# Moving weight loads, one weight conversion and parts of two scan units in a fused SSD scan and SiLU feed-forward kernel

## The chip, the core and the metric

The kernel runs on one core of a Trainium2 chip. The core has TensorE (PE in the profile, with PEld for its weight loads), VectorE (DVE), ScalarE (ACT), GpSimd (POOL) and SyncE (SP, which here only issues transfers); 16 DMA engines move data between HBM and SBUF. The metric is the device time of one execution in microseconds; lower is better. A kernel's time is the median of several runs, and the profile is one further execution.

## The reference

Two blocks one after the other. The first is a chunked state-space scan (Mamba-2's SSD) over 4 batches x 8 heads x 768 steps, with 32 values per head and 16 states; the second is a feed-forward layer on 3072 tokens of 256 values: a product with w_in (256 x 2048), SiLU, and a product with w_out (2048 x 256). All is float32.

```python
for c in range(nc):                       # chunks of the sequence
    cum = np.cumsum(la, axis=-1)          # la = log(clip(a, 1e-6, 1))
    L = np.exp(cum[:, :, :, None] - cum[:, :, None, :]) * causal
    CB = np.einsum('bhin,bhjn->bhij', Cc, Bc)
    y_intra = np.einsum('bhij,bhjd->bhid', CB * L, xc)
    y_inter = np.einsum('bhin,bhnd->bhid', Cc, state) * np.exp(cum)[:, :, :, None]
    y[:, :, sl] = y_intra + y_inter
    decay_from_j = np.exp(cum[:, :, -1:] - cum)
    Bx = np.einsum('bhjn,bhjd->bhjnd', Bc, xc) * decay_from_j[:, :, :, None, None]
    state = np.exp(np.sum(la, axis=-1))[:, :, None, None] * state + np.sum(Bx, axis=2)
x = y.transpose(0, 2, 1, 3).reshape(3072, 256)
h = x @ w_in
out = (h * (1.0 / (1.0 + np.exp(-h)))) @ w_out
```

## The kernel before

**Units.** The scan works in units of 256 steps of one batch, with chunks of 64 steps; units 0 to 2 are batch 0, unit 3 starts batch 1, twelve in all. A unit u takes these steps, each a function: `f_P` (DVE: running products of a from the tile pz, result pfx), `f_Ek` or `f_E1` (DVE: two scans that build the decay matrix E from the tile ab, one for each half k), `f_B` (B times the last column of E, result BT), `f_TP` or `f_T` (transposes of B and C into bh and ct, on TensorE or on DVE), `f_T2` (ACT: C for even and odd heads, ce), `f_C` (C times pfx, result cw), `f_G` (TensorE: C times B into a PSUM tile of four banks called gy or dp), `f_D0` (TensorE: BT times x), `f_M` (DVE: E times the products of `f_G`, written over E, for each half k), `f_S` (DVE: four states in a row, st), `f_SM` (ACT: copies of the states for even and odd heads, sm), `f_Y` (TensorE: the unit's output) and `f_X` (ACT: the output from PSUM into SBUF, xf).

**Weights.** w_in and w_out are taken in 16 blocks, n from 0: blocks 0 to 7 are 256 columns of w_in each, blocks 8 to 15 are 256 rows of w_out each. They arrive as float64, and the kernel makes float32 of them itself: `load_w(n)` brings 512 KB into a raw tile (a pool of six buffers, so block n + 6 waits until block n is converted), `w_size(n)` makes two tiles of it on ACT (wu from the upper words, wv from the lower), and `w_bits(n)` joins them with three DVE instructions and one addition, which is on POOL unless `adder` is DVE. In the program's text for the later blocks a step is one letter and a number: s is `w_size`, b is `w_bits`, a is `w_bits` with the addition on DVE, r is the load; h, l and d make the split parts of the weights with which the second phase computes.

**Order.** There is no scheduler: each engine executes its instructions in the order in which the program emits them. Phase one, to about 72 us, runs the scans of units 0 to 3 and the feed-forward of units 0 and 1 in plain float32: `f_s1(u, j)` is the product of unit u with block j into half a PSUM tile hp (two buffers) with SiLU on ACT behind it (gT), and `f_s2(j)` the product with block 8 + j. `busy(n)` issues n products of zeros, fillers whose result nobody reads. The text strings in `steps` say which steps of units 2 and 3 and of the weights follow each `f_s1`: "2:TB" is transposes and B of unit 2, "2:a" loads ab of unit 3. From 72 us a steady loop over the remaining unit pairs with split weights follows, which the change does not touch.

**Queues.** Nearly all loads go through SP, which issues them one by one in program order. `f_A2` (POOL) clips a of the later batches and `f_A3` stores it to scratch in HBM (a_in, a_zero), from where pz (`load_pa`) and ab (`load_ab`) of unit 3 and later are read back broadcast over partitions. In the stretch that the change touches SP's order before is: w4, x of unit 2, `f_A3`'s three stores, w5, B and C of unit 3 (eight loads, `load_bcx(3, "c")`), w6, pz and ab of unit 3, w7, B and x of unit 3, w8 and on.

Of the kernel before, what the change touches and what calls it, by code (L numbers as in the profile page):

```python
# [33 lines left out]
def kernel(  # L34
# [22 lines left out]
    nc = tc.nc  # L57

    batch, H, S, D = x.shape
# [26 lines left out]
    def block(name, dtype=FP32):  # L86

        return blk.tile([128, 512], dtype, name=name, tag="blk", bufs=NB)

    def half(name):  # L90
        return ps_h.tile([128, 512], FP32, name=name, tag="h")
# [46 lines left out]
    def load_x(u, q, ks=(0, 1)):  # L138
        b, t0 = at(u)
        if u not in xt:  # L140
            xt[u] = loads.tile([128, 2, H, D], FP32, name="xt", bufs=2)
        for k in ks:
            q.dma_start(out=xt[u][:, k], in_=x[b, :, t0 + 128 * k:t0 + 128 * k + 128].rearrange("h p d -> p h d"))
# [28 lines left out]
    def two(t):  # L172
        return t.rearrange("p (k f) -> p k f", k=2)

    def load_w(n, q):
        j = n % 8
        src = wi[:, :, j * WF:(j + 1) * WF] if n < 8 else wo[:, 2 * j:2 * j + 2]
        if src.dtype == FP32:
            w32[n] = block("w32")
            q.dma_start(out=two(w32[n]), in_=src)  # L180
            return
        t = raw[n] = quad.tile([128, 2, WF, 2], U32, name="raw", tag="quad")
        q.dma_start(out=t.rearrange("p k f two -> p k (f two)"), in_=src.bitcast(U32))
# [65 lines left out]
    load_n(0, 0, nc.scalar)  # L249
    load_a(0)  # L250
    load_x(0, nc.sync)
    for n in range(2):
        load_w(n, nc.sync)
    load_a(1)

    def f_A():
# [13 lines left out]
    def f_A2(first):  # L270

        r = slice(0, NC1)
        nc.gpsimd.tensor_scalar(out=(acl if first else acz)[r], in0=acl[r], scalar1=1.0, scalar2=1e-6, op0=ALU.min, op1=ALU.max)
        if not first:
            nc.gpsimd.memset(acz[r, :, 0:1], 0.0)

    def f_A3():

        r = slice(0, NC1)
        nc.sync.dma_start(out=a_in[:, :, 0:1].rearrange("h c t -> c h t"), in_=misc[r, 0:H].rearrange("p (h t) -> p h t", t=1))  # L280
        nc.sync.dma_start(out=a_in[:, :, 1:].rearrange("h c t -> c h t"), in_=acl[r])
        nc.sync.dma_start(out=a_zero, in_=acz[r])
# [12 lines left out]
    def busy(n, small=0, t=None):  # L295
        t = half("zero") if t is None else t
        for i in range(n):
            nc.tensor.matmul(out=t, lhsT=idle[:, 0:128], rhs=idle, start=True, stop=True)
        for i in range(small):
            nc.tensor.matmul(out=t[:64, :64], lhsT=idle[:, 0:64], rhs=idle[:, 64:128], start=True, stop=True)  # L300
# [67 lines left out]
    def f_Ek(u, k, hs=slice(0, H)):  # L368
        scan_E(u, H * k + hs.start, hs.stop - hs.start, ab.pop((u, k, hs.start))[:, hs])
# [8 lines left out]
    def f_B(u, engine=nc.vector, ks=slice(0, 2)):  # L378
        if u not in BT:
            BT[u] = sc.tile([128, 2, H, N], FP32, name="BT")  # L380
        engine.tensor_tensor(out=BT[u][:, ks], in0=bn[u][:, ks],
                             in1=E[u][:, ks, :, Q - 1:Q].to_broadcast([128, ks.stop - ks.start, H, N]), op=ALU.mult)
# [7 lines left out]
    def f_TP(u):  # L390

        d = new_dp(u)
        for i, t in enumerate((bn[u],) if u == 0 else (bn[u], tbc.pop(u))):
            for k in range(2):
                nc.tensor.transpose(out=d[:, 2 + i, 256 + 128 * k:384 + 128 * k],
                                    in_=t[:, k].rearrange("p h n -> p (h n)"), identity=ident)
        BH[u] = sc.tile([128, UT], FP32, name="bh")
        if u > 0:
            nc.scalar.activation(BH[u], d[:, 2, 256:512], AF.Copy)
        if u == 1:  # L400
            CT[u] = sc.tile([128, UT], FP32, name="ct")
            nc.scalar.activation(CT[u], d[:, 3, 256:512], AF.Copy)
        elif u > 0:
            CT[u] = d[:, 3, 256:512]
# [6 lines left out]
    def f_C(u, engine=nc.vector):  # L411
        CW[u] = sc.tile([128, UT], FP32, name="cw")
        engine.tensor_tensor(out=CW[u].rearrange("p (c t) -> p c t", t=Q),
                             in0=CT.pop(u).rearrange("p (c t) -> p c t", t=Q), in1=PFX[u][:, :, 1:], op=ALU.mult)
# [6 lines left out]
    def f_D0(u, ts=(0, 1, 2, 3)):  # L421
        last = u % UPB == UPB - 1
        bt = BT[u].rearrange("p k h n -> p k (h n)")
        xc = xt[u].rearrange("p k h d -> p k (h d)")
        if 0 < u <= UPB:
            d = [two(acc("d")[:, 0:128]) for c in range(2)]
        else:
            d = [two(new_dp(u)[:, c, 256:384]) for c in range(2)]
        for t in ts[:3 if last else 4]:
            k, c = divmod(t, 2)  # L430
            for g in range(4):
                nc.tensor.matmul(out=d[c][32 * g:32 * g + 32, k],
                                 lhsT=bt[64 * c:64 * c + 64, k, 32 * g:32 * g + 32],
                                 rhs=xc[64 * c:64 * c + 64, k, 64 * g:64 * g + 64], start=True, stop=True,
                                 tile_position=(64 * c, 32 * g), skip_group_check=True)
        BX[u] = d
        if 3 in ts:
            BT.pop(u)
# [61 lines left out]
    def f_X(u):  # L500

        XF[u] = block("xf")
        y = GY.pop(u)
        for w in range(2):
            nc.scalar.activation(two(XF[u])[:, w].rearrange("p (k c t) -> p c k t", k=2, c=2),  # L505
                                 y[:, 2 * w:2 * w + 2, 0:128].rearrange("p c (k t) -> p c k t", k=2), AF.Copy)
# [21 lines left out]

    GT, OA = {}, {}

    def f_s1(u, j):
        hp = two(half("hp"))
        for i in range(2):
            for kc in range(KC):
                nc.tensor.matmul(out=hp[:, i], lhsT=two(w32[j])[:, kc, 128 * i:128 * i + 128],  # L535
                                 rhs=two(XF[u])[:, kc], start=(kc == 0), stop=(kc == KC - 1))
        GT[u, j] = block("gT")
        nc.scalar.activation(two(GT[u, j]), hp, AF.Silu)
        if j == 7:
            XF.pop(u)  # L540
# [196 lines left out]
    w_size(1, "u")  # L737
    busy(2, 10)
    f_Y(0)
    busy(4)  # L740
    f_X(0)
    w_size(1, "v")
    load_w(4, nc.sync)
# [4 lines left out]
    for e in range(2):  # L748
        f_T2(1, e)
    f_Ek(1, 0)  # L750
    f_Ek(1, 1)
    f_s1(0, 0)
    f_B(1, nc.gpsimd)
    f_G(1)
    f_s1(0, 1)
    f_D0(1)
    f_M(1, 0)
    f_P(1)
    f_C(1, nc.gpsimd)
    f_P0(2, nc.gpsimd)  # L760
    f_A2(True)
    f_A2(False)
    f_A3()
    load_w(5, nc.sync)
    load_bcx(3, "c")
    load_w(6, nc.sync)
    load_pa(3, nc.sync)
    f_M(1, 1)
    w_size(2)
    f_S(1)  # L770
    f_SM(1)
    w_size(3, "u")
    busy(6)
    f_Y(1)
    f_X(1)
    w_size(3, "v")
    w_bits(2, adder=nc.vector)

    def stage(u, what):
        for c in what:  # L780
            if c == "L":
                load_unit(u)
            elif c == "a":
                load_ab(u + 1, nc.sync)
            elif c == "n":
                load_n(u, 0, nc.sync)
            elif c == "x":
                load_x(u, nc.sync)
            elif c == "T":
                if 0 < u < UPB:  # L790
                    f_TP(u)
                else:
                    f_T(u, 0)
                    f_T(u, 1)
                f_T2(u, 0)
                f_T2(u, 1)
            elif c == "P":
                f_P(u)
            elif c in "12":
                f_E1(u, int(c) - 1, 2)  # L800
            elif c == "B":
                f_B(u, nc.gpsimd if u == 2 else nc.vector)
            elif c == "C":
                f_C(u)
            elif c == "D":
                f_G(u)
                f_D0(u)
            elif c == "M":
                f_M(u, 0)
                f_M(u, 1)  # L810
            elif c == "S":
                f_S(u)
            elif c == "s":
                f_SM(u)
            elif c == "Y":
                f_Y(u)
                f_X(u)
            elif c == "h":
                f_xh(u)
            elif c == "l":  # L820
                f_xl(u)
            elif c == "d":
                f_xd(u)
# [4 lines left out]
    def todo(text):  # L828

        for step in text.split():  # L830
            if ":" in step:
# [3 lines left out]
            n = int(step[1:].split(".")[0])  # L835
            {"b": w_bits, "s": w_size, "h": w_h, "l": w_l, "d": w_d, "a": partial(w_bits, adder=nc.vector), "v": partial(w_d, vector=True), "m": f_s2, "p": s1_d, "r": load_r}[step[0]](n)

    steps = ((1, 0, "2:P12"), (1, 1, "2:TB a3 s4 2:a r7"), (0, 2, "2:CD 3:nx b4 s5 r8"), (1, 2, "2:SsM r9"),
             (0, 3, "b5 s6 r10"), (1, 3, "2:Y 3:T r11"), (0, 4, "3:P1 b6 s7 r12"), (1, 4, "3:C2B"), (0, 5, "b7 r13 s8"),
             (1, 5, "3:DSsM"), (0, 6, "b8 r14 s9"), (1, 6, "3:Y h0 l0"), (0, 7, "b9 r15 s10 s11"), (1, 7, "b10 s12 2:h"))  # L840
    for u, j, text in steps:
        f_s1(u, j)
        todo(text)
# [117 lines left out]
```

## Time and profile before

| What | Value |
| --- | --- |
| Three timed runs | 331.94, 333.86, 334.7 us |
| Their median | 333.86 us |
| Profiled execution, its time | 330.76 us |
| Its span, first to last instruction | 329.0 us |
| Mean granted TensorE clock | 0.998 |
| Moved by DMA, mean | 31.87 MB, 97 GB/s |

The page also cuts the span into 40 slices of 8.2 us; a digit is the busy share in tenths:

```profile
PE   8989999999999999999999999999999999999995
DVE  7989598987796988996866996866996863574443
ACT  3655669946688898667757657767657756656561
POOL 5532135785012131240202240202240202000000
PEclk9999999999999999999999999999999999999999
DMA  6997999797783952444600454600442000021001
```

The first eight slices hold what the change touches. A time given with an instruction below is its start in us from the start of the span. "A <- B" in a wait means that A's engine stood still until B, as far as the profile can tell; with several conditions it names the one that it saw come last, which can be another than the true one. On SP a line is the issuing of a transfer, not the transfer.

### The profile page before, as it was taken

Reading aid. Unit: us, or ns where it says so; the run is one execution under the profiler, and the core shown is the slowest. Engines: PE = TensorE matmul, PEld = TensorE weight load, DVE = VectorE, ACT = ScalarE, POOL = GpSimd, SP = SyncE. Lnnn points to the kernel's source line nnn. Section 1 sums busy time; section 2 is a strip of 40 time slices with the busy share of each in tenths; the row PEclk is TensorE's granted clock in tenths of the full one; section 3 lists DMA queues with packets and bytes.
Section 4 is the critical chain, followed back from the end, with each engine's and each line's share of the span. In section 5 each row is a group of like instructions: output and inputs, shape, how many; then the busy total and the mean of one; then the engine's idle time right before and its main releaser. Section 6 shows DMA issues by size and latency. Waiting matters only on the chain.

```text
span 329.0 us, 7993 instructions
## 1 busy us (share of the span) xinstructions
PE 321.2 (98%) x3226; PEld 260.5 (79%) x3229; DVE 251.4 (76%) x414; ACT 220.7 (67%) x422; POOL 76.5 (23%) x79
## 2 busy tenths in 40 slices
PE   8989999999999999999999999999999999999995
PEld 4557878888878788778788778788778788899995
DVE  7989598987796988996866996866996863574443
ACT  3655669946688898667757657767657756656561
POOL 5532135785012131240202240202240202000000
PEclk9999999999999999999999999999999999999999
DMA  6997999797783952444600454600442000021001
GB/s 132 242 188 192 226 287 292 153 183 134 159 139 84 160 99 53 99 73 100 118 3 0 84 95 92 119 3 0 94 86 49 2 2 0 0 36 31 2 0 64
DMA packets 92724, 31.87 MB, mean 97 GB/s; under 512 B 76480, under 2 KB 83392, under 8 KB 92688
## 3 DMA queue, kind: packets, MB, share of 16 engines
q1 hardware_dynamic: 87376, 25.60, 35.7%
q0 software_dynamic: 2944, 5.38, 9.1%
q10 hardware_dynamic: 2368, 0.39, 0.7%
q8 instruction: 25, 0.41, 0.6%
q14 instruction: 11, 0.09, 0.1%
HBM read 22.79 MB, written 3.32 MB: 79 GB/s over the span
## 4 chain that ended last, share of the span: by engine, by line
PE 87%; DMA 5%; DVE 4%; issue 2%; SPq 1%; POOL 1%; ACT 1%; DVEq 0%
PE hp L571 23%; PE hp L563 11%; PE oa L612 9%; PE oa L613 9%; PE b L643 9%; PE oa L548 8%; PE hp L535 3%; PE b L638 2%; PE b L621 2%; PE oa L621 2%; PE gy L495 2%; PE gy L446 2%; DMA bn<-in_B_dram 2%; DMA raw<-in_moe_w_in_dram 2%; PE gy L486 2%
## 5 line engine op out<-in xcount | busy, mean ns | idle before, releaser
L565 ACT ACTIVATE hp<-hp 128x512 f32<-128x512 f32 x80 | 46.6, 582 | 71.4 <-PE hp L563 71.3
L585 DVE TENSOR_TENSOR gl<-g,gh 128x512 fp32r<-128x512 f32 x62 | 42.7, 689 | 49.9 <-ACT gh L581 47.0
L571 PE MATMUL hp<-xh,wh 128*128 128x512 f32 x160 | 65.4, 408 | 0.0
L589 DVE SCALAR_TENSOR_TENSOR gd<-gh,g 128x512 fp32r<-128x512 f32 x80 | 59.5, 747 | 5.2 <-ACT gh L581 5.2
L571 PE MATMUL hp<-xl,wl 128*128 128x512 f32 x160 | 62.7, 392 | 0.0
L585 POOL TENSOR_TENSOR gl<-g,gh 128x512 fp32r<-128x512 f32 x18 | 29.3, 1630 | 121.7 <-ACT gh L581 115.8
L581 ACT ACTIVATE gh<-g 128x512 fp32r<-128x512 f32 x80 | 50.6, 632 | 2.8
L612 PE MATMUL oa<-gh,wh 128*128 128x512 f32 x128 | 50.0, 390 | 0.0
L613 PE MATMUL oa<-gl,wl 128*128 128x512 f32 x128 | 49.9, 390 | 0.0
L563 PE MATMUL hp<-xd,wd 128*128 128x512 f32 x160 | 49.6, 391 | 0.0
L579 ACT ACTIVATE g<-hp 128x512 f32<-128x512 f32 x80 | 47.5, 594 | 0.6 <-PE hp L571 0.6
L571 PEld LDWEIGHTS hp<-xh,wh 128*128 128x128 f32 x160 | 30.0, 188 | 8.8 <-ACT hp L565 2.6
L563 PEld LDWEIGHTS hp<-xd,wd 128*128 128x128 f32 x160 | 30.0, 188 | 6.6
L643 PE MATMUL b<-gd,wd 128*128 128x512 f32 x128 | 34.5, 389 | 0.0
L571 PEld LDWEIGHTS hp<-xl,wl 128*128 128x128 f32 x160 | 30.1, 188 | 4.8
L357 DVE TENSOR_TENSOR_SCAN E<-ab,diag 128x512 f32<-128x512 f32 (+1 forms) x26 | 29.4, 1165 | 1.9 <-DMA ab<-a_zero 1.6
L535 PE MATMUL hp<-xf,w 128*128 128x256 f32 x128 | 29.8, 385 | 0.6 <-ACT xf L505 0.5
L548 PE MATMUL oa<-gT,w 128*128 128x256 f32 x128 | 28.4, 379 | 0.0
L612 PEld LDWEIGHTS oa<-gh,wh 128*128 128x128 f32 x128 | 24.0, 188 | 5.1
L613 PEld LDWEIGHTS oa<-gl,wl 128*128 128x128 f32 x128 | 24.0, 188 | 5.1
L643 PEld LDWEIGHTS b<-gd,wd 128*128 128x128 f32 x128 | 24.0, 188 | 5.1
L535 PEld LDWEIGHTS hp<-xf,w 128*128 128x128 f32 x128 | 23.6, 190 | 4.5 <-ACT xf L505 0.6
(107 smaller groups left out, 460.0 us busy)
## 6 DMA issues: line engine op xcount, KB each, us to landing
ab<-a_zero SPq DMA_DIRECT2D x18, 256.0 KB
raw<-in_moe_w_in_dram SPq DMA_DIRECT2D x8, 512.0 KB
raw<-in_moe_w_out_dram SPq DMA_DIRECT2D x8, 512.0 KB
wl<-w POOLq DMA_DIRECT2D x16, 256.0 KB, 4.1
xt<-in_x_dram SPq DMA_DIRECT2D x24, 128.0 KB
out_dram<-ot SPq DMA_DIRECT2D x40, 64.0 KB
tbc<-in_C_dram SPq DMA_DIRECT2D x40, 32.0 KB
bn<-in_B_dram SPq DMA_DIRECT2D x20, 64.0 KB
```

The lines of the kernel that those rows point to most:

```text
L535: nc.tensor.matmul(out=hp[:, i], lhsT=two(w32[j])[:, kc, 128 * i:128 * i + 128], rhs=two(XF[u])[:, kc], start=(kc == 0), stop=(kc == KC - 1))
L548: nc.tensor.matmul(out=OA[0][m][:, UT * u:UT * u + UT], lhsT=two(w32[8 + j])[:, i, 128 * m:128 * m + 128], rhs=two(GT[u, j])[:, i], start= ...
L563: nc.tensor.matmul(out=HP[s], lhsT=two(WD[f // 2])[:, kc, 128 * (f % 2):128 * (f % 2) + 128], rhs=XD[P][:, kc], start=(kc == 0), stop=Fals ...
L565: nc.scalar.activation(HP[s], HP[s], AF.Copy, scale=HALF / UP)
L571: nc.tensor.matmul(out=HP[s], lhsT=two(w[f // 2])[:, kc, 128 * (f % 2):128 * (f % 2) + 128], rhs=x_[P][:, kc], start=False, stop=(kc == KC ...
L579: nc.scalar.activation(G[s], HP.pop(s), AF.Silu, scale=UP)
L581: nc.scalar.activation(GH[s], G[s], AF.Copy, scale=DOWN)
L585: engine.tensor_tensor(out=GL[s], in0=G[s], in1=GH[s].bitcast(FP32), op=ALU.subtract)
L589: nc.vector.scalar_tensor_tensor(out=GD[s], in0=GH[s].bitcast(FP32), scalar=1.0 + 1.0 / HALF, in1=G.pop(s), op0=ALU.mult, op1=ALU.subtract)
L612: nc.tensor.matmul(out=OA[P][m], lhsT=two(WH[n])[:, r, ms], rhs=gh, start=(f == 0), stop=False)
L613: nc.tensor.matmul(out=OA[P][m], lhsT=two(WL[n])[:, r, ms], rhs=gl, start=False, stop=(f == NF - 1))
L643: nc.tensor.matmul(out=B2[P][:, m], lhsT=two(WD[n])[:, r, 128 * m:128 * m + 128], rhs=gd, start=(fresh and s == tiles[0]), stop=True, skip ...
```

## The change

Seven edits, all in phase one:

- Unit 1's `f_B` is issued as two halves, each directly behind the scan that it needs, ahead of `f_s1(0, 0)`.
- Unit 1's `f_D0` is issued between the two halves of the product `f_s1(0, 1)`, not behind it; `f_s1` gets an argument for that.
- Fillers: six, not four, before `f_X(0)`; five, not six, before `f_Y(1)`; two new ones before `f_X(1)`.
- Unit 2's transposed C is copied from PSUM to SBUF on ACT, as unit 1's was, and `f_C(2)` moves from DVE to POOL, directly behind `f_B(2)`.
- SP's order: w5 ahead of the three stores of a; w6 and w7 ahead of B and C of unit 3 (before: w6 behind them, w7 behind ab of unit 3).
- `w_bits(6)` does its addition on DVE, not on POOL.
- `w_size(8)` and `w_size(9)` each move one product later: behind `f_SM(3)` and behind `f_X(3)`.

The first hunk only writes a loop out; it changes no instruction.

```diff
-    for n in range(2):
-        load_w(n, nc.sync)
+    load_w(0, nc.sync)
+    load_w(1, nc.sync)
...
-        if u == 1:
+        if u in (1, 2):
             CT[u] = sc.tile([128, UT], FP32, name="ct")
             nc.scalar.activation(CT[u], d[:, 3, 256:512], AF.Copy)
...
-    def f_s1(u, j):
+    def f_s1(u, j, between=None):
         hp = two(half("hp"))
         for i in range(2):
+            if i == 1 and between:
+                between()
             for kc in range(KC):
...
     f_Y(0)
-    busy(4)
+    busy(6)
     f_X(0)
...
     f_Ek(1, 0)
+    f_B(1, nc.gpsimd, slice(0, 1))
     f_Ek(1, 1)
+    f_B(1, nc.gpsimd, slice(1, 2))
     f_s1(0, 0)
-    f_B(1, nc.gpsimd)
     f_G(1)
-    f_s1(0, 1)
-    f_D0(1)
+    f_s1(0, 1, lambda: f_D0(1))
...
     f_A2(False)
+    load_w(5, nc.sync)
     f_A3()
-    load_w(5, nc.sync)
+    load_w(6, nc.sync)
+    load_w(7, nc.sync)
     load_bcx(3, "c")
-    load_w(6, nc.sync)
     load_pa(3, nc.sync)
...
-    busy(6)
+    busy(5)
     f_Y(1)
+    busy(2)
     f_X(1)
...
-                f_C(u)
+                f_C(u, nc.gpsimd if u == 2 else nc.vector)
...
-    steps = ((1, 0, "2:P12"), (1, 1, "2:TB a3 s4 2:a r7"), (0, 2, "2:CD 3:nx b4 s5 r8"), (1, 2, "2:SsM r9"),
-             (0, 3, "b5 s6 r10"), (1, 3, "2:Y 3:T r11"), (0, 4, "3:P1 b6 s7 r12"), (1, 4, "3:C2B"), (0, 5, "b7 r13 s8"),
-             (1, 5, "3:DSsM"), (0, 6, "b8 r14 s9"), (1, 6, "3:Y h0 l0"), (0, 7, "b9 r15 s10 s11"), (1, 7, "b10 s12 2:h"))
+    steps = ((1, 0, "2:P12"), (1, 1, "2:TBC a3 s4 2:a"), (0, 2, "2:D 3:nx b4 s5 r8"), (1, 2, "2:SsM r9"),
+             (0, 3, "b5 s6 r10"), (1, 3, "2:Y 3:T r11"), (0, 4, "3:P1 a6 s7 r12"), (1, 4, "3:C2B"), (0, 5, "b7 r13"),
+             (1, 5, "3:DSsM s8"), (0, 6, "b8 r14"), (1, 6, "3:Y s9 h0 l0"), (0, 7, "b9 r15 s10 s11"), (1, 7, "b10 s12 2:h"))
```

## The prediction

> **What bounds the kernel now.** I read the page first, then the busy time by stretch, then the waits of TensorE, then the order of time on each engine around those waits. The page:
>
> ```profile
> PE 321.2 (98%) x3226; PEld 260.5 (79%) x3229; DVE 251.4 (76%) x414; ACT 220.7 (67%) x422; POOL 76.5 (23%) x79
> ```
>
> TensorE is busy 321.2 of 329.0 us, so at most 7.8 us could be won. The table by stretch (PE, PEld, DVE, ACT, POOL busy, granted clock, DMA share, GB/s) says where:
>
> ```profile
> 0.00:24.00 24.00, 20.27 (x384) 12.81 (x388) 20.64 (x47) 12.48 (x27) 12.66 (x28) 1.00 0.89 188
> 24.00:60.00 36.00, 35.56 (x446) 29.60 (x445) 30.42 (x52) 26.21 (x53) 11.71 (x10) 1.00 0.89 242
> 60.00:324.00 264.00, 263.90 (x2389) 216.83 (x2388) 198.87 (x313) 181.24 (x343) 52.17 (x42) 1.00 0.37 69
> ```
>
> Idle: 3.73 us before 24, 0.44 us from 24 to 60, 0.10 us from 60 to 324, and 3.51 us in the last 5 us (the tail, untouched). The change lies between 12 and 55 us; there the waits of TensorE are (us in total, times, longest)
>
> ```profile
> PE gy L486 <- POOL pz L345: 1.1, 1, 1.1
> PE gy L395 <- DMA bn<-in_B_dram: 0.5, 1, 0.5
> PE hp L535 <- ACT xf L505: 0.5, 1, 0.5
> PE gy L446 <- DVE cw L413: 0.3, 1, 0.3
> ```
>
> In the order of time these are 0.48 us before unit 1's transposes (13.85), 1.08 before f_Y(1) (21.64), 0.47 before f_s1(1, 0) (23.59) and 0.34 before f_G(2) (29.82); a fifth, 0.09 us, is the idle rest of 42 to 46 (3.91 busy of 4.00). Sum 2.46 us: the most the change can remove from this execution, 0.7%. DVE, ACT and the queues count only where they would open a new wait.
>
> **Unit 1's B in halves, D0 within a product.** ACT and DVE beside TensorE (start, us, instruction, idle before):
>
> ```profile
> 18.81 0.60 ACT L538 ACTIVATE gT<-hp 128x512 f32<-128x512 f32 x1 [2.05 <-PE hp L535]
> 19.86 0.68 ACT L192 ACTIVATE wv<-raw 128x512 f32<-128x512 uint32 x1
> 20.84 0.69 ACT L473 ACTIVATE sm<-st,par 128x128 f32<-128x128 f32 x2 [0.30 <-DVE st L466]
> 18.04 0.69 DVE L452 TENSOR_TENSOR E<-gy,E 128x512 f32<-128x512 f32 x1 [0.80 <-POOL BT L381]
> ```
>
> The wait before f_Y(1) is put down to POOL's pz, which had ended at 21.31; what ends last at 21.53 is ACT's sm, so I take sm. It waits for the states (DVE), which stand behind f_M(1, 0), which waits for POOL's BT (17.37 to 18.01) because M writes over the E that BT reads. With halves, the first needs only the first scan (over at 16.08) and follows w's second half at 16.49; the second needs the scan that ends at 17.24. A half's price: POOL's L208 takes 754 ns at 256 columns and 1359 at 512, so 149 fixed and 605 per 256; BT's 656 then gives 0.40 each, 0.15 more in all, hidden under the scans. M starts at 17.27, 0.77 sooner. D0 inside the product can start after half of L535's 1.89 us, at 16.78 + 0.95 = 17.73, with BT's second half ready at 17.37 + 0.40 = 17.77: nearly no wait. f_S(1) then runs behind f_M(1, 1), ready about 0.77 sooner, at 20.36.
>
> But D0's 0.39 us (18.70 to 19.09) now delays the end of that product, so silu's gT moves from 18.81 to 19.20; ACT's wu and wv behind it occupy 0.49, 0.56 and 0.57 us each start to start, which brings sm to 19.20 + 0.49 + 0.56 + 0.57 = 20.82, against 20.84. ACT replaces DVE as what comes last: f_Y(1) stays at 21.64. Gain 0.0; bounds: 0.3 better (the idle time at sm, if D0 cost nothing) and 0.4 worse (D0's length). The value is computed from rows right there.
>
> **Fillers.** A filler is about 0.22 us start to start (six in 19.09 to 20.3). Two more before unit 1's transposes are 0.44 us in a wait of 0.48 for the load of B: nothing; if B landed first, 0.44 is on the path. One fewer before f_Y(1), two after it: 0.44 in the 0.47 us before f_s1(1, 0), which waits for ACT's xf either way: nothing, and 0.44 if that wait were gone.
>
> **C of unit 2 copied, cw on POOL.** One ACT copy more (0.38 us; L402), cw (0.41 us) off DVE, 0.70 us onto POOL, which sat idle from 27.83 to 31.25. f_G(2) no longer waits for cw behind DVE's conversion but for ACT's ce: bh 27.84, ct 28.11, ce from 28.38, over by about 29.25, and the product before G ends at 29.48. So this 0.34 us goes; ACT's block behind ce is 0.27 later, in front of a gT with spare time. Bound: if ACT were late by a whole copy, 0.04 of gain remain.
>
> The Trainium skill, page "SBUF — State Buffer", section "Who interferes with whom", speaks against cw on POOL and for the next edit: a VectorE instruction with two SBUF inputs and a GpSimd instruction that reads SBUF exclude each other for their whole length. By that rule cw on POOL could hold DVE up for its whole length; it would change the sum by nothing, as the cover below is longer.
>
> The row that bears on it is the next fence: a scan of two SBUF tiles took 2.29 us while POOL's L208 ran from 42.72 to 44.10, and 1.22 us alone. DVE loses at most 0.70 - 0.41 = 0.29 us by cw's move; its output is due at Y(2) (36.19), and sm(2) is over at 34.4: 1.8 us of cover.
>
> **Block 6's last addition on DVE, and the loads.** What gates unit 3:
>
> ```profile
> 40.04 1.22 DVE L357 TENSOR_TENSOR_SCAN E<-ab,diag 128x512 f32<-128x512 f32 x1 [1.63 <-DMA ab<-a_zero]
> 42.90 2.29 DVE L357 TENSOR_TENSOR_SCAN E<-ab,diag 128x512 f32<-128x512 f32 x1
> 45.22 0.42 DVE L381 TENSOR_TENSOR BT<-bn,E 128x256 f32<-128x256 f32 x1
> 42.72 1.38 POOL L208 TENSOR_TENSOR w<-wu,wv 128x512 uint32<-128x512 uint32 x1 [6.79 <-DVE wv L206]
> 45.06 0.69 PE L446 MATMUL gy<-ce,bh 32*64 32x128 f32 x32
> 45.70 0.46 PE L432 MATMUL d<-xt,BT 64*32 64x64 f32 x32
> ```
>
> D0(3) starts 0.06 us after BT(3) ends, with no idle time before it: no slack at all, so whatever TensorE gains ahead is kept only if BT(3) comes sooner too. Putting L208 on DVE costs 0.61 there (0.69 in the rows, start to start 0.61) and takes POOL's instruction away from the second scan: 2.29 to 1.2, so 1.09 less. From the landing of ab to BT's end: 5.60 before, 5.60 + 0.61 - 1.09 = 5.12 after.
>
> When does ab(3) land? SP issues the same instructions up to x of unit 2 (24.39). Then w5 (0.45 us) precedes a's store (3.16 us), so the store is out at about 28.0, w6 and w7 at 28.9, the eight B, C loads of unit 3 at 33.2 and pa(3) at 33.3 to 33.4, before 33.45: in time the same. What is new is 512 KB of w7 in front of pa(3) and ab(3). At 238 GB/s (34 to 42 us) that is 2.20 us; but from 31 to 34 the DMA share was only 0.31, so 2.07 us of transfer time lay empty, and w6 and w7 now stand issued before it. ab(3) lands 0.13 later, at 40.17; BT(3) ends at 45.29, D0(3) starts at 45.35, 0.35 sooner. Nothing in SP's new queue waits for a buffer: w6 and w7 need blocks 0 and 1 converted (by 15.0). Behind them wait B, C of unit 3 (transposed on DVE at 34.50, probably at 36 now, into DVE's own wait of 2.11 us for pz) and pa(3).
>
> w7 landing some 5 us sooner ends the 0.09 wait near 43, where a load that landed at 41.30 led to the gT that freed the next product's bank; ACT's waits for w5, w6, w7 (1.50, 1.17, 1.10) shrink, worth nothing more, since TensorE did not wait there.
>
> **s8 and s9 later.** Two conversions of 1.24 us on ACT move behind sm(3) and X(3). ACT stood idle 2.01 us before s8 (45.69), so 1.24 us of work moves from idle time into its full stretch from 51 to 67.6: everything there is about 1.0 later. Covers: w32[8] ready at 52.3, read at 54.59; w32[9] at 55.6, read at 58.0; xd of unit 3 ends at 69.4, the first product that reads it starts at 71.67. The least cover is 2.3 us, less 1.0, less the lead of TensorE: 0.9 us remain. Nothing; if DVE's 98% from 60 to 70 turned that into 2.3 or more, the excess would be on the path.
>
> **Sum.** Removed: 0.34 and 0.09; D0(3) lets 0.35 through. The load and cover terms are good to some 0.1, so 0.4 us. Own time of the profiled execution: 330.76 - 0.4 = 330.4. The three timed runs lie 1.2 to 3.9 us above that execution and average 333.50; the stages are the same, so I take 333.50 - 0.4 = 333.1.
>
> **Rivals.** (1) Faster: the timed runs' surplus over the profiled execution is waiting for loads, which this change mostly brings forward. Then all 2.46 us go: 333.86 - 2.46 = 331.4. For: the 13.85 and 43 us waits end with a DMA. Against: two of the five waits end with ACT's own work. (2) Slower, one mechanism: unit 3's ab sits behind w7 and the empty transfer time is not filled (small transfers of B, C or a's store stretch instead). ab lands at 40.04 + 2.20 = 42.24, BT(3) ends at 47.36, D0(3) starts at 47.42 instead of 45.70: +1.7 us, 335.6. It decides from a landing past 40.52 (45.64 - 5.12). For: DMA share 1.00 from 34 to 42. Against: the 0.31.
>
> The Trainium skill, page "DMA: Bandwidth & Descriptors", section "Queues, rings and completion order", sides with the rival: descriptors on each ring are consumed in the order issued. Taken alone it would give the rival's time; of the empty stretch it says nothing.
>
> (3) The change does not do what it says: the waits that fillers cover are not there in the timed runs; 0.44 + 0.44 on the path, less 0.4: 333.50 + 0.5 = 334.0.
>
> **Chances.** Forecast 0.60; rival 1 0.16, rival 2 0.16, rival 3 0.08. The range goes from 330.4 (the profiled execution's own forecast, beyond rival 1) to 335.6 (rival 2). About 1%, 3.3 us, is what a measurement of this kernel can tell from no change (its three runs spread over 2.8 us). Faster by over 1%, below 330.5, needs rival 1 and more: 0.09. Slower by over 1%, above 337.2, needs rival 2 with pz late as well: 0.09. Within: 0.82.
>
> **What would show it.** f_M(1, 0) near 17.3 and f_S(1) over by 20.4, but sm(1) still at 20.8 behind ACT's wv; no wait before G(2); the second scan of unit 3 at 1.2 us; DMA share near 0.9 from 31 to 34; ab(3) landing at 40.2 and D0(3) at 45.3; no TensorE idle time from 60 to 324. I am wrong if D0(3) comes after 45.7, if ACT lets sm start before 20.5, or if the first product on xd waits at 71.

## Result, and the profile after

| | Before | After |
| --- | --- | --- |
| Median, 20 runs each | 333.26 us | 336.25 us |
| Lowest to highest | 330.75 to 334.70 us | 333.76 to 338.58 us |
| After over before, 95% interval | | 1.0093 [1.0067, 1.0118] |
| Profiled execution, its time | 330.76 us | 335.41 us |
| Its span | 329.0 us | 333.7 us |
| Mean granted TensorE clock in it | 0.998 | 0.992 |

The kernel became 0.9% slower; the forecast was 0.4 us less. The ratios, here and below, leave out runs more than 1.5% above the fastest of the same kernel, which matters chiefly for one experiment, the load order done by itself, where it leaves out seven of 12 runs. Line numbers of the changed kernel from `f_s1` on are two higher (L535 is now L537, silu's gT L538 is L540). The page:

```profile
PE 324.3 (97%) x3232; PEld 262.1 (79%) x3232; DVE 250.2 (75%) x414; ACT 221.1 (66%) x423; POOL 76.6 (23%) x80
```

TensorE is 3.1 us busier for almost the same instructions (three fillers of 0.22 us are 0.66 of it): something ran at a lower clock. The table by stretch (PE, PEld, DVE, ACT, POOL busy, granted clock, DMA share, GB/s) shows where:

```profile
0.00:24.00 24.00, 21.20 (x389) 13.04 (x390) 20.92 (x48) 12.02 (x27) 13.71 (x29) 1.00 0.89 186
24.00:60.00 36.00, 32.86 (x425) 27.13 (x425) 23.80 (x45) 21.81 (x46) 7.81 (x8) 0.95 0.79 213
60.00:324.00 264.00, 263.99 (x2371) 216.03 (x2371) 201.42 (x316) 185.00 (x349) 55.11 (x44) 1.00 0.38 73
```

The loss is all between 24 and 60 us: 3.14 us of idle time instead of 0.44, and a mean clock of 0.95. The steady loop is as it was. The waits of TensorE from 8 to 75 us (us in total, times, longest) are now three, and one is most of them (a time in which TensorE stands still is called a stand below):

```profile
PE d L432 <- DVE BT L381: 3.1, 1, 3.1
PE gy L486 <- POOL pz L345: 1.3, 1, 1.3
PE gy L432 <- DVE BT L381: 0.2, 1, 0.2
```

That wait stands before `f_D0(3)`. TensorE around it, in order of time (start, us, instruction, idle before):

```profile
44.59 0.69 PE L446 MATMUL gy<-ce,bh 32*64 32x128 f32 x32
48.41 0.46 PE L432 MATMUL d<-xt,BT 64*32 64x64 f32 x32 [3.13 <-DVE BT L381]
48.80 5.38 PE L537 MATMUL hp<-xf,w 128*128 128x256 f32 x16
```

G(3) comes 0.47 us sooner than before (45.06), D0(3) 2.71 later (45.70). The 16 products behind it take 5.38 us where such a group takes 3.72, so 1.66 more. Two stretches in the same columns as the table above: the second shows the granted clock, 0.50, behind the stand; to the first, with a DMA share of 0.20, the text comes back.

```profile
36.00:38.00 2.00, 2.00 (x100) 1.74 (x100) 0.25 (x1) 1.72 (x5) 0.49 (x1) 1.00 0.20 51
...
49.00:50.00 1.00, 1.00 (x3) 0.82 (x4) 0.90 (x4) 0.00 (x0) 0.17 (x1) 0.50 0.97 272
```

2.71 + 1.66 = 4.37 of the 4.7 us by which the two spans differ. On DVE, what D0(3) waits for:

```profile
43.10 1.23 DVE L357 TENSOR_TENSOR_SCAN E<-ab,diag 128x512 f32<-128x512 f32 x1 [2.10 <-DMA ab<-a_zero]
...
46.68 1.22 DVE L357 TENSOR_TENSOR_SCAN E<-ab,diag 128x512 f32<-128x512 f32 x1
47.93 0.42 DVE L381 TENSOR_TENSOR BT<-bn,E 128x256 f32<-128x256 f32 x1
```

The second scan is down from 2.29 to 1.22, as intended, but the first one starts at 43.10 instead of 40.04, because ab lands at 43.0. Why it lands late is on SP (start and us of the issuing, not of the transfer):

```profile
28.69 0.91 SPq L183 DMA_DIRECT2D raw<-in_moe_w_in_dram  x2
29.65 2.82 SPq L135 DMA_DIRECT2D tbc<-in_B_dram  x4
32.79 4.38 SPq L135 DMA_DIRECT2D tbc<-in_C_dram  x4
37.22 0.63 SPq L106 DMA_DIRECT2D pz<-a_in  x1
37.95 1.26 SPq L113 DMA_DIRECT2D ab<-a_zero  x2
```

Before, pz was issued at 33.45 and ab at 34.18. Now eight small loads keep SP from 29.65 to 37.17, and the DMA engines run dry meanwhile: their share from 36 to 38 is 0.20, shown above, where it was 0.99. SP's own waits from 28 to 40 us put a name to it:

```profile
SPq L135 <- DMA raw<-in_moe_w_in_dram: 3.6, 3, 2.0
SPq L135 <- DMA a_in<-misc: 0.6, 1, 0.6
```

B and C wait for the landing of *weights*, and of a store of a, which they neither read nor write. The trace records the semaphores of each instruction: SP's transfers raise one of eight semaphores, taken in turn, and an issue first waits on the one that it will raise, that is, for the landing of the transfer eight places ahead of it in SP's order. The eight are this program's own, and stand in its instructions. Counted from w5 the order is w5 (1), a's three stores (2 to 4), w6 (5), w7 (6), B (7 to 10), C (11 to 14), pz (15), ab (16, 17). So B's third load waits for w5, its fourth for a's first store, C's third for w6 and C's fourth for w7. The three that wait for a weight were issued at 31.26, 35.57 and 36.86, and by the same records w5, w6 and w7 had landed at 31.24, 35.55 and 36.84, each 0.02 us ahead. ACT, whose conversion of a block waits for the same landing, agrees: it started on block 6 at 35.58, 0.01 us after C's third load went out:

```profile
35.58 0.67 ACT L189 ACTIVATE wu<-raw 128x512 f32<-128x512 f32 x1 [0.55 <-DMA raw<-in_moe_w_in_dram]
```

**Main theory**: w6 and w7 stand within eight places ahead of C, so SP is held until each of them has landed, and pz and ab, queued behind C, go out 3.8 us late. **Rivals**: the 512 KB more ahead of ab are what delays it (bytes, the prediction's second rival); the other edits of the change cost the time; and the low clock is a disturbance of its own and not a consequence of the stand.

### The profile page after: what moved, and what is told of

Read it like the earlier page. It is cut to its first block, busy times and chain, and to the rows that moved or that the text cites. A ratio compares the mean times of both kernels' runs of the same rounds, so it can differ in the third digit from the quotient of the medians.

```text
span 333.7 us, 8000 instructions
## 1 busy us (share of the span) xinstructions
PE 324.3 (97%) x3232; PEld 262.1 (79%) x3232; DVE 250.2 (75%) x414; ACT 221.1 (66%) x423; POOL 76.6 (23%) x80
## 3 DMA queue, kind: packets, MB, share of 16 engines
q0 software_dynamic: 2944, 5.38, 9.3%
## 4 chain that ended last, share of the span: by engine, by line
PE 85%; DMA 7%; SPq 4%; DVE 2%; issue 1%; POOL 0%; DVEq 0%
PE hp L573 23%; PE hp L565 11%; PE oa L614 9%; PE oa L615 9%; PE b L645 9%; PE oa L550 8%; PE hp L537 3%; PE gy L495 2%; PE b L640 2%; PE b L623 2%; PE oa L623 2%; SPq L143 2%; PE gy L486 2%; DMA pa<-in_a_dram 2%; DMA tbc<-in_B_dram 2%; PE gy L446 2%
## 5 line engine op out<-in xcount | busy, mean ns | idle before, releaser
L537 PE MATMUL hp<-xf,w 128*128 128x256 f32 x128 | 31.5, 400 | 0.0
L357 DVE TENSOR_TENSOR_SCAN E<-ab,diag 128x512 f32<-128x512 f32 (+1 forms) x26 | 28.3, 1124 | 2.9 <-DMA ab<-a_zero 2.1
L537 PEld LDWEIGHTS hp<-xf,w 128*128 128x128 f32 x128 | 24.7, 199 | 4.6 <-ACT xf L505 0.5
```

## Experiments

Ratios are against the kernel before in the same series, with 95% intervals. Its median was 333.00 us in the series of the load order undone, the load order done alone, the loads on POOL and the fillers in the stand; 333.46 in that of pz and ab first, w7 back, the head's sm first and block 6's addition; and 333.65 in that of the other three. Between series the ratios are the better comparison.

**Load order alone undone.** All other edits stay.

```diff
     f_A2(False)
-    load_w(5, nc.sync)
     f_A3()
-    load_w(6, nc.sync)
-    load_w(7, nc.sync)
+    load_w(5, nc.sync)
     load_bcx(3, "c")
+    load_w(6, nc.sync)
     load_pa(3, nc.sync)
...
-(1, 1, "2:TBC a3 s4 2:a")
+(1, 1, "2:TBC a3 s4 2:a r7")
```

> The changed kernel with SP's old order of loads (w5 behind the stores of a, w6 behind B and C of unit 3, w7 behind ab); all else as changed. Main theory: SP keeps eight transfers outstanding, each issue waits for the one eight before it; in the changed kernel the last two loads of C stand eight behind w6 and w7 and hold pz and ab of unit 3 back, so D0(3) is late and TensorE stands. It expects pz issued near 33.5, ab landed near 40, no wait before D0(3) over 0.5 us, granted clock over 0.995, and a time 0.2 to 1.0 us under the kernel before (332.3 to 333.1). Rival A, bytes: w7's 512 KB in front of ab on the rings: the same here. Rival B, the rest of the change (s8 and s9 later on ACT, addition 6 on DVE): D0(3) stays late by 2 us or more and the time over 335.5.

Measured: median 332.35 us (331.60 to 333.88, 12 runs), ratio 0.9974 [0.9947, 1.0000]; profiled span 329.6, clock 1.0. pz went out at 33.16, ab landed at 40.31, and D0(3) started without a wait, the products behind it at full clock:

```profile
45.88 0.45 PE L432 MATMUL d<-xt,BT 64*32 64x64 f32 x32
46.26 3.72 PE L537 MATMUL hp<-xf,w 128*128 128x256 f32 x16
```

The whole loss goes with the load order, so the other edits do not carry it.

**Load order alone done**, in the kernel before.

```diff
     f_A2(False)
+    load_w(5, nc.sync)
     f_A3()
-    load_w(5, nc.sync)
+    load_w(6, nc.sync)
+    load_w(7, nc.sync)
     load_bcx(3, "c")
-    load_w(6, nc.sync)
...
-(1, 1, "2:TB a3 s4 2:a r7")
+(1, 1, "2:TB a3 s4 2:a")
```

> The kernel before with nothing but the new order of loads. Main theory: pz issued near 37, ab landed near 43, and as the second scan still waits for POOL's addition, BT(3) ends 5.6 us later, 48.6: TensorE stands some 2.9 us or more, the clock falls, and the time is 336.0 to 338.5. Rival A: the same. Rival B: 332.8 to 333.8, no wait before D0(3).

Measured: median 338.58 us (332.96 to 341.08 but for one run at 529.14; 12 runs), ratio 1.0054 [1.0002, 1.0107]; the median says more here. Profiled span 336.7, clock 0.989: pz out at 37.98, ab landed at 44.34, the second scan back at 2.28 beside POOL, and

```profile
49.98 0.68 PE L432 MATMUL d<-xt,BT 64*32 64x64 f32 x32 [4.00 <-DVE BT L381]
50.60 6.52 PE L535 MATMUL hp<-xf,w 128*128 128x256 f32 x16
```

A longer stand than in the changed kernel, and behind it 6.52 us for the 16 products: the load order alone brings both the stand and the low clock.

**w6 and w7 issued by POOL**, which takes them out of SP's turn of eight but leaves their bytes ahead of ab.

```diff
-    load_w(6, nc.sync)
-    load_w(7, nc.sync)
+    load_w(6, nc.gpsimd)
+    load_w(7, nc.gpsimd)
```

> The changed kernel with w6 and w7 issued from POOL's queue at the same place of the program (on POOL that is behind the clipping of a, near 24 us): the same bytes leave ahead of pz and ab of unit 3, earlier even, but they are not among SP's eight. Main theory: pz issued by 33.5, ab landed by 40.5, no wait over 0.5 us before D0(3), 332.0 to 333.3. Rival A, bytes: ab lands at 42 or later, D0(3) waits 1.5 us or more, 334.5 or more. Rival B: as the changed kernel, 336.

Measured: 333.72 us (331.44 to 336.24), ratio 1.0009 [0.9976, 1.0043]; span 331.2, clock 1.0. pz went out at 36.44 and ab landed at 42.55, later than the theory said; D0(3) waited 0.79, and x of unit 2 came late as well (a wait of 1.08 before D0(2)). POOL issues the two loads from 24.66 on, ahead of w5 (26.40 on SP). SP's issue of w5 then ended at 29.56 and w5 landed at 33.84, where the changed kernel and the four runs that share its order up to there (fillers, pz and ab first, four loads moved, w7 back) have 27.20 to 27.76 and 30.95 to 31.81, and everything behind it moved. Here the traffic in flight does slow things, so this run meets neither theory's numbers and tells them apart badly.

**pz and ab directly behind w7**, B and C behind them: the same bytes stand ahead of ab's issue as weights, but nothing that waits for a weight's landing stands between.

```diff
     load_w(7, nc.sync)
-    load_bcx(3, "c")
     load_pa(3, nc.sync)
...
+            elif c == "t":
+                load_bcx(u, "c")
...
-(1, 1, "2:TBC a3 s4 2:a")
+(1, 1, "2:TBC a3 s4 2:a 3:t")
```

> The changed kernel with pz and ab of unit 3 issued directly behind w6 and w7, and B and C of unit 3 behind them: the 512 KB each of w6 and w7 still stand in front of pz and ab, but pz is only two places behind w6, so no wait for w6 or w7 holds it. Main theory (the wait for the transfer eight places back): pz issued by 33, once a's store has landed (32.1 in the changed kernel), ab landed by 40; now the last loads of B and C stand eight behind w6 and w7, C lands at 39 to 40.5, BT(3) ends at 45.5 to 46.5, the wait before D0(3) is under 1.3 us, clock 0.998 or more, 332.5 to 334.2. Rival A, bytes in front of ab on the rings: ab at 42.5 or later, the wait 2.5 us or more, 335.5 or more.

Measured: 334.76 us (331.70 to 337.80), ratio 1.0002 [0.9971, 1.0033]; in the profile, which is of the slowest of the 12 runs, pz went out at 32.84, and the second half of ab had landed by 40.82, when C's fourth load, eight places behind it, was issued. So ab lands 2.2 us sooner than in the changed kernel with w6 and w7 still ahead of it: the bytes are not what held it. But the time missed the expected gain, because the hold moved onto C. C's first load now stands eight behind w7 and went out at 38.92; ACT's ce(3) was late by that, a gT stood behind it on ACT, and TensorE stood for the gT instead, in this execution at least:

```profile
44.96 6.75 PE L537 MATMUL hp<-xf,w 128*128 128x256 f32 x16 [3.39 <-ACT gT L540]
```

**Four loads moved.** If the turn of eight is the cause, it is enough to shift C out of reach of w6 and w7: with B's four loads ahead of w6, the eighth place behind w6 is the second half of ab, and behind w7 it is bn. w6 and w7 remain wholly ahead of pz and ab.

```diff
     f_A3()
+    load_t(3, 0, nc.sync)
     load_w(6, nc.sync)
     load_w(7, nc.sync)
-    load_bcx(3, "c")
+    load_t(3, 1, nc.sync)
```

> The changed kernel with the four loads of B of unit 3 ahead of w6 and w7, the four of C behind them: w6 and w7 still stand with all their bytes in front of C, pz and ab, but only the second half of ab is eight places behind w6. Main theory: pz issued at 34 to 35.5 instead of 37.2, ab landed at 40 to 41.5 instead of 43.0, D0(3) near 45.5 to 46.5, clock 0.998 or more, 332.3 to 333.8. Rival A (bytes in front): w6 and w7 leave later than in the changed kernel, so ab lands at 43 or later and the time is 336 or more.

Measured: 332.19 us (331.48 to 334.07, 12 runs), ratio 0.9974 [0.9944, 1.0004]; span 329.8, clock 1.0. SP and DVE:

```profile
32.17 2.24 SPq L135 DMA_DIRECT2D tbc<-in_C_dram  x4
34.45 0.62 SPq L106 DMA_DIRECT2D pz<-a_in  x1
```

```profile
40.80 1.23 DVE L357 TENSOR_TENSOR_SCAN E<-ab,diag 128x512 f32<-128x512 f32 x1 [0.96 <-DMA ab<-a_zero]
```

C takes 2.24 us of SP, not 4.38, ab lands 2.3 us sooner than in the changed kernel, D0(3) waits 0.77 (at 46.11) and no half clock follows. From 336.25 to 332.19, 4.1 us (1.2% by the ratios), for an order that moves four loads of 32 KB and no weight relative to ab. This is the run that decides between the count and the bytes.

**w7 alone back behind ab.**

```diff
     load_w(6, nc.sync)
-    load_w(7, nc.sync)
     load_bcx(3, "c")
...
-(1, 1, "2:TBC a3 s4 2:a")
+(1, 1, "2:TBC a3 s4 2:a r7")
```

> The changed kernel with only w7 back behind ab of unit 3; w6 stays ahead of B and C. Main theory: the last load of C is eight places behind w6 and waits for it (near 33.5 to 34.5), pz issued at 34 to 35 instead of 37.2, ab landed at 40.3 to 41.5, the wait before D0(3) 0 to 1.2 us, 332.5 to 334.0. Rival A (bytes): w6's bytes stand in front of ab as before the change, so ab at 40 and pz at 33.5 as before. Rival B (rest of the change): 335.5 or more.

Measured: 332.78 us (331.00 to 336.37, 10 runs), ratio 0.9981 [0.9948, 1.0014]. C's fourth load is now eight behind w6: pz out at 35.19, between the old order's 33.16 and the changed kernel's 37.22; ab landed at 41.21. No wait before D0(3), but 1.05 us for a gT at 44.38 because block 7 arrives later. Bytes would fit this run as well; only beside the previous one does it speak for the count.

**Fillers in the stand**: the stand stays, but TensorE is kept at work in it.

```diff
                 f_G(u)
+                if u == 3:
+                    busy(14)
                 f_D0(u)
```

> The changed kernel with 14 fillers between G(3) and D0(3), that is in the 3.1 us in which TensorE stood in the changed kernel; 14 x 0.22 = 3.0 us. Theory: after the stand the granted clock was 0.50 from 49 to 52 us and the products took twice their time, 1.7 us lost; with the fillers the clock stays at 1.00 there, D0(3) still comes near 48.4, and the time falls by 1.0 to 1.7 us to 334.5 to 335.3. Rival: the low clock does not come from the stand; then the time stays at 336.3 or rises.

```profile
45.55 3.19 PE L298 MATMUL zero<-misc 128*128 128x512 bf16 x13
48.67 0.45 PE L432 MATMUL d<-xt,BT 64*32 64x64 f32 x32
49.06 3.72 PE L537 MATMUL hp<-xf,w 128*128 128x256 f32 x16
```

Measured: 334.85 us (334.16 to 335.82), ratio 1.0046 [1.0019, 1.0073]. The records show 13 of the 14 fillers. D0(3) is no sooner (48.67), but here the fillers hold it: BT(3) was ready at 47.05. The products take 3.72 again, and the time is 1.4 us below the changed kernel's (0.5% by the ratios). All 12 runs were granted 0.998 or more of the clock, and 16 of the changed kernel's 20 runs 0.995 or less. So the low clock comes from TensorE standing, not from ab being late as such, and costs about 1.4 us; whether fewer fillers would have won more was not tried.

**The head (the stretch up to about 24 us): sm(1) ahead of block 2's conversion**, on the first experiment's kernel. It tests what ends last before Y(1), which the trace puts down to POOL's pz and the prediction to ACT's sm.

```diff
-    w_size(2)
     f_S(1)
     f_SM(1)
+    w_size(2)
     w_size(3, "u")
-    busy(5)
+    busy(4)
     f_Y(1)
```

> e1 (the changed kernel with SP's old order) with block 2's conversion on ACT moved behind sm(1), and four fillers, not five, in front of Y(1). In e1 and in the changed kernel DVE had the states ready at 20.3 but sm(1) began only at 20.95 behind ACT's wu and wv: the halves of B and D0 within the product gained nothing at Y(1). If that reading is right, sm(1) begins at 20.3 to 20.5, Y(1) some 0.6 earlier, at 21.1 to 21.3; block 2 is converted 0.7 later, with cover to 27.8. The lead may be lost again at D0(3), which waits for ab: time 0 to 0.6 us under e1's 332.35, so 331.7 to 332.4. Rival: Y(1) waits for something else (pz on POOL, as the profile names it) and stays at 21.7; time as e1.

Measured: 332.75 us (331.60 to 334.34), ratio 0.9979 [0.9952, 1.0006]. ACT's sm starts at 20.45 and Y(1) at 21.24, 0.60 sooner than the 21.84 of the first experiment, so Y(1) did hang on ACT; POOL's pz, which the trace names, began only at 22.41 in this run, when Y(1) was already at work. The lead is lost two steps on, in a wait of 1.90 us for ACT's xf (product at 24.94), behind ACT's own wait of 1.67 us for block 3 to land. Time as without it: a miss.

**Block 6's addition back on POOL**, on the first experiment's kernel.

```diff
-(0, 4, "3:P1 a6 s7 r12")
+(0, 4, "3:P1 b6 s7 r12")
```

> e1 with block 6's addition back on POOL. Theory: POOL's addition holds the second scan of unit 3 up again (2.2 to 2.3 us instead of 1.22), BT(3) ends 0.3 to 0.6 later than e1's 45.57 and D0(3) waits 0 to 0.5 us: time 0 to 0.5 us over e1, 332.3 to 332.9. Rival: that addition cost nothing or more on DVE: the scan stays near 1.2, time as e1 or under it.

Measured: 332.99 us (331.48 to 333.95, 10 runs), ratio 0.9970 [0.9939, 1.0000]; the second scan is 2.29 us again. The median is 0.6 us above the first experiment's, but the two come from different series and their ratios are the same (0.9970 and 0.9974). The 1.07 us of the scan are real, and 0.35 us of them is left once the addition itself is on DVE (from the start of the first scan to BT's end 5.26 us, and 5.61 here); their worth in the kernel's time is not resolved.

**The head's edits alone** (units 1 and 2 and the fillers, in the kernel before).

```diff
-            (0, 4, "3:P1 a6 s7 r12"), (1, 4, "3:C2B"), (0, 5, "b7 r13"),
-            (1, 5, "3:DSsM s8"), (0, 6, "b8 r14"), (1, 6, "3:Y s9 h0 l0")
+            (0, 4, "3:P1 b6 s7 r12"), (1, 4, "3:C2B"), (0, 5, "b7 r13 s8"),
+            (1, 5, "3:DSsM"), (0, 6, "b8 r14 s9"), (1, 6, "3:Y h0 l0")
```

(shown against the first experiment's kernel, from which it differs by this)

> The kernel before with the changes to units 1 and 2 and the fillers alone (B in halves, D0 within the product, C of unit 2 copied, cw on POOL); SP's old order, block 6's addition on POOL, conversions of blocks 8 and 9 in their old places. Theory: the whole gain of e1 comes from here, that of G(2)'s wait; D0(3) may take some of it back: 332.2 to 333.2, ratio 0.995 to 1.000. Rival: e1's gain comes from the addition on DVE or from blocks 8 and 9; then this is as before, ratio 0.999 to 1.003.

Measured: 333.47 us (332.39 to 335.88, 10 runs), ratio 0.9997 [0.9963, 1.0030]. Not to be told from before. What the first experiment gains, at the edge of its interval, is therefore not pinned on these edits. The clock is another candidate, though no run singles it out: in the first experiment's series the kernel before was granted 0.995 or less in 10 of 35 runs, the first experiment in none of 12, and the runs granted more have medians of 332.52 and 332.35 us.

**A try at something better**: the head with sm(1) first, as above, with w6 and w7 both behind ab, and blocks 3, 6 and 7 converted later.

```diff
     load_bcx(3, "c")
-    load_w(6, nc.sync)
...
-(1, 1, "2:TBC a3 s4 2:a r7")
+(1, 1, "2:TBC a3 s4 2:a r6 r7")
...
-(0, 3, "b5 s6 r10"), (1, 3, "2:Y 3:T r11"), (0, 4, "3:P1 a6 s7 r12"), (1, 4, "3:C2B")
+(0, 3, "b5 r10"), (1, 3, "2:Y 3:T s6 r11"), (0, 4, "3:P1 a6 r12"), (1, 4, "3:C2B s7")
```

The diff leaves out the head, where `w_size(2)` stands behind `f_SM(1)`, four fillers stand before `f_Y(1)`, two behind it, and all of `w_size(3)` behind `f_X(1)`.

> A version meant to beat both kernels, from e1: sm(1) ahead of block 2's conversion, block 3's conversion behind X(1), w6 and w7 behind pz and ab of unit 3, blocks 6 and 7 converted later on ACT (behind ce of unit 3, and one product later). Theory: Y(1) at 21.2 and the product behind X(1) at 23.0 to 23.3 instead of 23.8; ab landed near 38 to 39, so BT(3) ends by 44.5 and D0(3) does not wait; no wait of a product for gT over 0.3 us: 331.2 to 332.2, 0.5 to 1.2 us under e1's 332.35. Rival: the lead is lost again in a later wait (w6 or w7 landing late for block 6 or 7, or gT behind them): 332.3 or more.

Measured: 334.13 us (333.08 to 337.43), ratio 1.0010 [0.9977, 1.0042]. The head came out as expected (Y(1) at 21.33, the product behind xf at 23.29), but the lead met the loads: ACT waited 2.51 us for w5 and 1.21 for w6, and TensorE 1.16 and 0.91 us for the gT behind them (35.05 and 43.02). No version that was run beats the kernel before by more than its interval.

## Why the prediction was wrong

**The failing step** is the one on the loads: "w6 and w7 at 28.9, the eight B, C loads of unit 3 at 33.2 and pa(3) at 33.3 to 33.4, before 33.45: in time the same", with "Nothing in SP's new queue waits for a buffer". The eight loads began at 29.65, 0.75 us later than foretold, and ended at 37.17, not 33.2, so that pz went out at 37.22 and not at 33.3 to 33.4. Buffers were indeed free; SP waited for semaphores, each tied to the transfer eight places back. I read each queue for buffers and bytes and did not count places. The profile of before had shown it: a wait of 0.8 us of B and C's line for a weight's landing (C's fourth load, eight behind w5), which a load of C has no reason to have. Such a wait between unrelated tiles was the clue.

From that step the rest of the sum falls: ab(3) "0.13 later, at 40.17" landed at 43.0, and D0(3) "at 45.35" came at 48.41.

**Rival 2** had the right place and nearly the right landing (42.24 against 43.0) and the right threshold, with the wrong mechanism. Its own counter-argument, the empty transfer time, held: the DMA share from 31 to 34 went from 0.31 to 0.93, so the bytes did find room. It also stopped at 335.6 because no step priced what a long stand does to the clock: 1.66 us in the profile, 1.4 in the run with fillers. The stages of the loss, by ratio: the other edits -0.26% (load order undone), the late ab +0.72% (1.0046 less 0.9974), the clock +0.47% (1.0093 less 1.0046), each good to some 0.4%. The stage of the late ab takes in the fillers, which held D0(3) in the profile.

The Trainium skill, page "DMA: Bandwidth & Descriptors", section "Queues, rings and completion order", on which the prediction weighed that rival, is about the order in which the descriptors on a ring are consumed; the hold measured here, 3.8 us at pz, is ahead of that, at the issuing.

**Steps that held**:

- The head in halves gains nothing: f_M(1, 0) at 17.27 (17.27 foretold), S(1) over at 20.3 (20.36), sm(1) at 20.95 (20.82), Y(1) at 21.73 (21.64). That ACT's sm ends last there was shown by moving it.
- The wait of 0.34 before G(2) is gone; together with the 0.09 TensorE reaches G(3) 0.47 sooner, where 0.43 was foretold.
- Block 6 on DVE: second scan 1.22 (1.2 foretold); from ab's landing to BT's end about 5.25 us instead of 5.60, foretold 5.12.
- The two conversions moved later cost nothing: TensorE is busy 263.99 of 264 us from 60 to 324.

**The other rivals.** That all waits fall (rival 1) is out. Fillers on the path (rival 3) are not seen: the head's edits alone measured 0.9997, though its interval of 0.3% either way would not show the 0.5 us of that rival, and in the profile of the changed kernel the products behind them start at 14.16 and 23.78 (14.23 and 23.59 before), so at most 0.2 us is lost there. The base of 333.50 was good; 20 runs of before have the median 333.26. What sets the timed runs above the profiled execution, which rival 1 took for waiting on loads, may in part be the clock: in the experiments' three series the kernel before was granted 0.995 or less in 41 of 99 runs (where in them, no profile shows), and 0.998 in its profile.

With the places counted, the forecast would have had pz and D0(3) late; by how much (2.71 us here) hangs on when w6 and w7 land, which no row of before gives. The clock's share could not have been taken from the profile of before, which has no such stand.

## What to carry to other kernels

A queue's issue order has a second cost besides bytes and buffers: with a fixed number of transfers outstanding (eight on SP here, by the program's semaphores), a large load holds up whatever stands that many places behind it, however small and unrelated. Before moving loads, number the queue and ask of each urgent transfer what stands eight ahead of it; four small loads moved were worth 4.1 us here. Price a stand of TensorE of some 3 us at its length and the half clock behind it (5.38 us for 3.72 us of products in the changed kernel), and if it can't be removed, fill it.

## What the runs showed of the hardware

- **The clock after a stand.** Stands of 3.13, 3.39 and 4.00 us (the changed kernel, pz and ab first, the load order alone) were each followed by a granted clock near 0.50 and by 16 products of 5.38, 6.75 and 6.52 us instead of 3.72. Stands of 1.90 us (sm(1) first) and of 2.05 us (the head alone, before a product at 26.75) were followed by 3.72. Of the changed kernel's 20 runs the three at clock 1.0 took 334.02 to 334.39 us, the three at 0.989 337.42 to 338.58.
- **When it falls.** In all thirteen profiles the record of the granted clock, from its first rise on, is made of steps of 3.41 us: full speed held for 11, 13 or 95 to 97 of them until its first fall, and the half clock in mid-kernel for one (changed kernel, 48.78 to 52.20) or two (load order alone, 49.47 to 56.30; pz and ab first, 44.33 to 51.16). So the clock is set anew once in 3.41 us, and what counts is the work of TensorE within a step. The step of the changed kernel that holds its stand, and the next (same columns as above):

```profile
45.37:48.78 3.41, 0.37 (x32) 0.30 (x32) 3.31 (x7) 0.00 (x0) 0.00 (x0) 1.00 1.04 346
48.78:52.20 3.42, 3.42 (x21) 2.75 (x9) 3.15 (x8) 1.20 (x4) 1.26 (x1) 0.50 0.98 313
```

  As the profile dates TensorE's work, the clock fell behind every whole step at full clock with 1.54 us of it or less (0.37 here, 0.00 with the load order alone, 0.65 with pz and ab first, and six steps at the ends of spans) and behind none with 1.55 us or more; that exact edge is of these thirteen executions alone. At half clock, steps with 2.90 us (load order alone) and 2.78 us (pz and ab first) of work did not bring it back; full ones did. The stand of 2.05 us lay across two steps and left 2.02 and 1.61 us of work in them. The steps lie elsewhere in each execution, so the same stand can cost none, one or two of them. The changed kernel's 20 runs fit that: four at 0.998 or more, thirteen at 0.992 to 0.995 and three at 0.989 (one step at half clock in 334 us makes 0.995, two make 0.990).
- The Trainium skill, page "TensorE: Matmul & The Clock Gate", section "HAM oscillation — how this bites in real kernels", warns of gaps of TensorE above about 3.4 us. Here a stand of 3.13 us was not spared: the measurement puts the edge lower.
- **An issue itself can take long.** SP's issue of one 512 KB load took 0.37 to 0.6 us in quiet stretches. That of w5 took 1.18, 1.67, 1.96, 2.93 and 3.20 us in the changed kernel and the four runs that share its order up to there, but ended between 27.20 and 27.76 us in all five, and at 29.56 with the two loads in flight that POOL had begun to issue 1.7 us ahead of it. What SP waits for there stays open.
